# One order for all five engines, worked out by a list scheduler inside the kernel, in place of an order of matmuls written out by hand

## The chip, the cores and the metric

The kernel runs on one core of one Trainium2 chip. Such a core has five engines with queues of their own: TensorE (PE, matrix products into PSUM), VectorE (DVE), ScalarE (ACT), GpSimd (POOL) and SyncE (SP, which here issues every DMA). Each works through its own list of instructions strictly in order, and semaphores join the lists. The metric is the device time of one execution in microseconds (us), as a median over runs. A profile of one execution shows every instruction, what ended the idle time before it, and the TensorE clock that was granted.

## What is computed

Two layers. The first is a linear attention with decay, over 4 batches, 8 heads, 768 positions and 48 channels a head; the second a feed-forward layer of width 2048 with a squared ReLU, on the 3072 rows of 384 that the first gives.

```python
for t in range(S):
    cur = np.einsum('bhd,bhe->bhde', u[None] * kt, vt)
    y[:, :, t] = np.einsum('bhd,bhde->bhe', rt, state + cur)
    state = wt[:, :, :, None] * state + np.einsum('bhd,bhe->bhde', kt, vt)
x = attn_out.transpose(0, 2, 1, 3).reshape(B * S, H * D)
h = x @ w_in
r = np.maximum(h, 0.0)
out = (r * r) @ w_out
```

## The kernel before

**Steps.** Attention works on chunks of 128 positions of one batch: 6 chunks times 4 batches are 24 steps. A step loads `w`, `r`, `k` and `v` (192 KB each; L67 to L80). Its parts, with the letters that the order uses:

- `st_prep` (L144): on ACT, the logarithm of `w` into one of three `lw` buffers, and `v` cast to bf16.
- `c`, `st_cum` (L164): PE sums the logarithms along the chunk by a triangular product into the PSUM tile `cp`; ACT takes the exponent there (and of the four columns of chunk sums, `a_c`); DVE multiplies it with `r` and `k` into `rdec` (L177).
- `t`, `st_tr` (L181): eight transposes on PE into PSUM `tr`, which DVE copies to `rkT` (L189). With it goes `st_bonus` (L153), the term of `u`: POOL makes `ku` and `qprod`, DVE the sum `q` (L160), POOL `vq`.
- `p`, `st_p` (L212): products of the transposed `r` and `k`, into the same PSUM buffer `cp`; DVE masks both halves into `pmT` (L223).
- `s`, `st_su` (L191): the chunk's part of the state, into `tr`; DVE adds the old state, POOL scales it into `S` (L208). The state goes from step to step, within a batch.
- `y`, `st_y` (L227): masked products with `v`, and the state with `rkT`, into PSUM `y`; DVE adds `vq` and gives `y_sb` (L245).
- `x`, `finish` (L320): three transposes of `y_sb` into `tr`; ACT copies them into `xT` (L256).

**Products.** When the steps of a block are in `xT`, `moe_block` (L259) has its feed-forward work as units. A unit `m1` fills one PSUM bank with 512 columns of the hidden layer (6 matmuls of 256 rows in a block of two steps, 12 of 128 rows in a block of one step); ACT takes the ReLU into `rl` (L276), and DVE squares it into `gt` (L277). A unit `m2` is a quarter of the second product for 128 rows, 4 matmuls; after four of them ACT evicts `o_sb` (L291) and SP stores it (L292). There are thirteen blocks: steps 0 and 1, 2, 3, and then pairs from 4 and 5 to 22 and 23.

**Weights.** `w_in` and `w_out` come as four blocks of 768 KB each into a pool of five staging buffers, and ACT casts each block in one instruction (L100, L103).

**PSUM.** One buffer each for `cp` (two banks), `y` (two banks), `tr` and `m2` (one each) and two for `m1` fill the eight banks.

**Order.** Only the order on PE is written out (`manual_schedule` for the tensor engine, L364): strings of letters, in which `F` takes the next unit of a queue of fills. From step 3 on a step reads `c(t+1) F F x(t-1) F F t(t+1) p(t) F F s(t+1) F F y(t)`, with fewer `F` early. The units `m1` of a block alternate with the units `m2` of the block before; `LAG` holds a new block back by two fills. The other engines are ordered by the framework's own scheduler, from the order in which the instructions are written. `ahead` (L334) asks for loads up to `PF` = 8 steps ahead, into pools of 9 buffers. Loads and stores share SP's queue.

```python
f = ["F F"] * 4 if t > 8 else ["F F", "F F", "F F", "F"] if t > 5 else ["F"] * 4 if t == 3 else ["F", "", "F", ""]
run(f"c{t + 1} {f[0]}" + (f" x{t - 1}" if t > 3 else "") +
    f" {f[1]} t{t + 1} p{t} {f[2]} s{t + 1} {f[3]} y{t}")
```

Of the kernel before, what the change touches and what calls it, by code (L numbers as in the profile page):

```python
# [9 lines left out]
FP32 = mybir.dt.float32  # L10
# [7 lines left out]
def kernel(  # L18
# [11 lines left out]
    nc = tc.nc  # L30
# [14 lines left out]
    PF = 8  # L45
    LAG = 2
# [5 lines left out]
    stage_pool = ctx.enter_context(tc.tile_pool(name="stage", bufs=5))  # L52
    a_in = ctx.enter_context(tc.tile_pool(name="a_in", bufs=9))
# [45 lines left out]
    def cast_wi(g):  # L99
        nc.scalar.copy(wi_sb[:, :, g * GW:(g + 1) * GW], w_st.pop(("i", g))[:])  # L100

    def cast_wo(g):
        nc.scalar.copy(wo_sb[:, g * 4:(g + 1) * 4, :], w_st.pop(("o", g))[:])  # L103

    loads = {0: attn_load(0)}

    u_bc = consts.tile([C, H, D], FP32)
    nc.sync.dma_start(
        out=u_bc[:],
        in_=bass.AP(tensor=u.tensor, offset=u.offset,  # L110
                    ap=[[0, C]] + [list(x) for x in u.ap]))
# [13 lines left out]
    nc.vector.memset(ones_col[:], 1.0)  # L125

# [14 lines left out]
    states = {}  # L141
    S_of = {}

    def st_prep(step):  # L144

        ld = loads.pop(step)
        st = states[step] = dict(ld)
        lw = st["lw"] = lw_bufs[step % NLW]
        nc.scalar.activation(lw[:, :, 0:D], ld["w_raw"][:], AF.Ln)
        v_bf = st["v_bf"] = a_mid.tile([C, H, D], BF16, name="v_bf", bufs=3)  # L150
        nc.scalar.copy(v_bf[:], ld["v_raw"][:])  # L151

    def st_bonus(step):  # L153
        st = states[step]
        ku = a_mid.tile([C, H, D], FP32, name="ku")
        qprod = a_mid.tile([C, H, D], FP32, name="qprod")
        nc.gpsimd.tensor_mul(ku[:], st["rk_raw"][:, 1], u_bc[:])  # L157
        nc.gpsimd.tensor_mul(qprod[:], st["rk_raw"][:, 0], ku[:])  # L158
        q = a_small.tile([C, H], FP32, name="q")
        nc.vector.reduce_sum(q[:], qprod[:], axis=AX.X)  # L160
        vq = st["vq"] = a_mid.tile([C, H, D], FP32, name="vq", bufs=3)
        nc.gpsimd.tensor_mul(vq[:], st["v_raw"][:], q[:, :, None].to_broadcast([C, H, D]))  # L162

    def st_cum(step):  # L164
        st = states[step]
        lw = st["lw"]
        cs = ps_cp.tile([C, 2, 512], FP32, name="cp")
        for p in range(HP):
# [4 lines left out]
        a_c = st["a_c"] = a_small.tile([C, HP], FP32, name="a_c")  # L173
        nc.scalar.activation(a_c[:], cs[:, 0, DM:DM + HP], AF.Exp)
        nc.scalar.activation(cs[:, :, 0:DM], cs[:, :, 0:DM], AF.Exp)  # L175
        rdec = st["rdec"] = rdec_bufs[step % NRD]
        nc.vector.tensor_mul(  # L177
            rdec[:, :, :, 0:D], st["rk_raw"][:],
            cs[:, :, 0:DM].rearrange("p a (h d) -> p a h d", h=H))

    def st_tr(step):  # L181
        st = states[step]
        rdec = st["rdec"]
        ps_tr = ps_tr_pool.tile([C, 2, HP, C], BF16, name="tr")
        rkT = st["rkT"] = a_mid.tile([C, 2, HP, C], BF16, name="rkT")
        for i in range(2):
            for p in range(HP):
                nc.tensor.transpose(ps_tr[:, i, p, :], rdec[:, i, 2 * p:2 * p + 2, :], ident[:])  # L188
        nc.vector.tensor_copy(rkT[:], ps_tr[:])  # L189

    def st_su(step):  # L191
        st = states[step]
        rdec, v_bf = st["rdec"], st["v_bf"]
        c = step % NCH
        if c == NCH - 1:
            return
        ps_su = ps_tr_pool.tile([C, HP, D], FP32, name="tr")
        for p in range(HP):
            for e in range(2):
                nc.tensor.matmul(ps_su[e * DP:(e + 1) * DP, p, :], rdec[:, 1, 2 * p + e, :],  # L200
                                 v_bf[:, 2 * p + e, :], start=True, stop=True)
        t_state = a_mid.tile([C, HP, D], FP32, name="t_state")
        if c == 0:
            nc.vector.tensor_copy(t_state[:], ps_su[:])
        else:
            nc.vector.tensor_add(t_state[:], S_of[step][:], ps_su[:])  # L206
        S_new = a_mid.tile([C, HP, D], BF16, name="S", bufs=3)
        nc.gpsimd.tensor_mul(S_new[:], t_state[:],  # L208
                             st["a_c"][:, :, None].to_broadcast([C, HP, D]))
        S_of[step + 1] = S_new  # L210

    def st_p(step):  # L212
        st = states[step]
        rkT = st["rkT"]
        ps_p = ps_cp.tile([C, 2, 512], FP32, name="cp")
        pmT = st["pmT"] = a_mid.tile([C, 2, HP, C], BF16, name="pmT")
        for p in range(HP):
            for e in range(2):
# [188 lines left out]
```

## Time and profile before

| | |
|---|---|
| median of 3 runs | 233.93 us (233.86 to 234.52) |
| the profiled execution | 234.28 us |
| its span, first to last instruction | 232.5 us |
| mean granted TensorE clock | 0.955 |
| first matmul of a feed-forward unit | at 26.52 us |
| share of span in which PE was busy | 84% |
| moved by DMA | 30.42 MB |

The page of the profile gives busy time for each engine, the span in 40 slices of 5.8 us, and groups of instructions. A busy PE is not PE at its peak: matmuls overlap, and the end of each is modelled, so that the price of a unit is read from the distance between starts. `PEld` is the loading of stationary operands, which lies beside the matmuls. A group row gives the sum and the mean of one; a row of the timeline gives start, length, engine, line, operation, tiles, and in brackets the idle time ahead of it with what ended it. `SPq` rows are DMA issues: their length is the time that the queue took to accept the transfer.

### The profile page before, as it was taken

To read this page: it belongs to the slowest core of one execution; us is meant where nothing else is said; L and a number is where in the kernel's file an instruction comes from. 1 tells how busy PE (TensorE), PEld (TensorE's weight loads), DVE (VectorE), ACT (ScalarE), POOL (GpSimd) and SP (SyncE) were. 2 spreads that over 40 slices of the span, in tenths; PEclk is the share of its full clock that TensorE was granted. 3 is DMA by queue.
4 is the path that set the end of the run, shared out by engine and by line. 5 is a ranking of instruction groups with operands and counts; after the bars stand their busy time and mean duration, and the time that the engine had idled before them with its cause. 6 is when DMAs were issued, how large, how long until landed. Compare 5 with 4: busy or idle time off the path is not lost.

```text
span 232.5 us, 5432 instructions
## 1 busy us (share of the span) xinstructions
PE 194.8 (84%) x2120; PEld 141.3 (61%) x2120; DVE 143.0 (61%) x264; ACT 131.4 (57%) x249; POOL 81.2 (35%) x105
## 2 busy tenths in 40 slices
PE   0145694794787999989999999999999999999984
PEld 0023472663465677767777777777777777777742
DVE  2244356235567688796879878987677756753210
ACT  2338479274245558547655775567755664455530
POOL 4450410547525855357626563431211120000000
PEclk9999997589569999999999999999999999999999
DMA  7999998999999999998785561010001000101001
GB/s 137 206 344 280 327 295 163 190 171 189 187 206 216 174 199 194 220 184 166 141 167 113 110 126 37 34 36 3 35 34 38 35 3 34 37 34 37 34 34 68
DMA packets 107176, 30.42 MB, mean 131 GB/s; under 512 B 100368, under 2 KB 105616, under 8 KB 107152
## 3 DMA queue, kind: packets, MB, share of 16 engines
q1 hardware_dynamic: 107152, 30.09, 63.0%
q8 instruction: 16, 0.26, 0.5%
q14 instruction: 8, 0.07, 0.1%
HBM read 25.36 MB, written 4.72 MB: 129 GB/s over the span
## 4 chain that ended last, share of the span: by engine, by line
PE 56%; SPq 14%; DVE 8%; DMA 7%; POOL 6%; issue 4%; ACT 3%; POOLq 0%; DVEq 0%; ACTq 0%
SPq L68 13%; PE tr L188 4%; DMA rk_raw<-in_k_dram 4%; PE cp L220 2%; DVE pmT L223 2%; POOL qprod L158 2%; POOL ku L157 2%; DVE rkT L189 2%; DMA u_bc<-in_u_dram 2%; DMA v_raw<-in_v_dram 2%; DVE gt L277 1%; PE y L234 1%; PE tr L255 1%; PE cp L171 1%; PE m_3691 L287 1%
## 5 line engine op out<-in xcount | busy, mean ns | idle before, releaser
L277 DVE TENSOR_TENSOR gt<-rl 128x512 bf16<-128x512 f16 x96 | 48.1, 509 | 34.2 <-ACT rl L276 33.8
L272 PEld LDWEIGHTS <-wi_sb 128*128 128x128 bf16 x624 | 57.2, 102 | 15.4 <-issue 3.4
L287 PEld LDWEIGHTS <-gt 128*128 128x128 bf16 x384 | 37.4, 99 | 18.6 <-issue 2.7
L208 POOL TENSOR_TENSOR S<-t_state,a_c 128x192 bf16<-128x192 f32 x20 | 10.5, 525 | 72.6 <-DVE t_state L206 56.3
L223 DVE TENSOR_TENSOR pmT<-cp,tri_strict 128x512 bf16<-128x512 f32 x48 | 30.7, 679 | 2.5 <-PE cp L220 2.5
L162 POOL TENSOR_TENSOR vq<-v_raw,q 128x384 f32<-128x384 f32 x24 | 20.0, 833 | 32.8 <-DVE y_sb L245 18.9
L160 DVE TENSOR_REDUCE q<-qprod 128x8 f32<-128x384 f32 x24 | 13.2, 549 | 21.5 <-POOL qprod L158 13.9
L157 POOL TENSOR_TENSOR ku<-rk_raw,u_bc 128x384 f32<-128x384 f32 x24 | 24.4, 1018 | 4.6 <-DMA u_bc<-in_u_dram 4.6
L158 POOL TENSOR_TENSOR qprod<-rk_raw,ku 128x384 f32<-128x384 f32 x24 | 24.4, 1018 | 3.1 <-DVE q L160 1.3
L151 ACT CAST v_bf<-v_raw 128x384 bf16<-128x384 f32 x24 | 12.2, 510 | 15.4 <-PE y L234 8.8
L189 DVE COPY rkT<-tr 128x1024 bf16<-128x1024 bf16 x24 | 16.4, 685 | 5.7 <-PE tr L188 5.4
L175 ACT ACTIVATE cp<-cp 128x768 f32<-128x768 f32 x24 | 19.2, 799 | 0.5 <-DVE q L160 0.2
L245 DVE TENSOR_TENSOR y_sb<-vq,y 128x384 bf16<-128x384 f32 x24 | 13.2, 551 | 2.2 <-PE y L234 1.1
L256 ACT COPY xT<-tr 128x384 bf16<-128x384 bf16 x24 | 11.4, 476 | 3.4 <-PE tr L255 3.3
L220 PE MATMUL cp<-rkT 64*128 64x128 bf16 x192 | 10.6, 237 | 3.0 <-DVE rkT L189 3.0
L234 PEld LDWEIGHTS <-pmT 128*128 128x128 bf16 x192 | 8.9, 101 | 6.8 <-DVE pmT L223 4.4
L234 PE MATMUL y<-v_bf,pmT 128*128 128x48 bf16 x192 | 10.6, 191 | 2.8 <-DVE pmT L223 2.7
L177 DVE TENSOR_TENSOR rdec_buf_159<-rk_raw,cp 128x768 bf16<-128x768 f32 x8 | 7.6, 952 | 6.5 <-ACT cp L175 5.1
L255 PE MATMUL tr<-ident,y_sb 128*128 128x128 bf16 x72 | 8.6, 234 | 2.4 <-DVE y_sb L245 1.6
L220 PEld LDWEIGHTS <-rkT 64*128 64x128 bf16 x192 | 6.0, 101 | 6.2 <-DVE rkT L189 3.4
L188 PE MATMUL tr<-ident,rdec_buf_157 128*128 128x128 bf16 x64 | 5.7, 242 | 4.7 <-DVE rdec_buf_157 L177 4.7
L255 PEld LDWEIGHTS <-y_sb 128*128 128x128 bf16 x72 | 6.0, 103 | 5.9 <-DVE y_sb L245 2.8
(295 smaller groups left out, 362.8 us busy)
## 6 DMA issues: line engine op xcount, KB each, us to landing
w_raw<-in_w_dram SPq DMA_DIRECT2D x24, 192.0 KB, 4.4
rk_raw<-in_r_dram SPq DMA_DIRECT2D x24, 192.0 KB, 4.5
rk_raw<-in_k_dram SPq DMA_DIRECT2D x24, 192.0 KB, 4.6
v_raw<-in_v_dram SPq DMA_DIRECT2D x24, 192.0 KB, 4.0
out_dram<-o_sb SPq DMA_DIRECT2D x24, 192.0 KB, 2.0
w_st<-in_moe_w_in_dram SPq DMA_DIRECT2D x4, 768.0 KB, 8.0
w_st<-in_moe_w_out_dram SPq DMA_DIRECT2D x4, 768.0 KB, 9.3
u_bc<-in_u_dram SPq DMA_DIRECT2D x1, 192.0 KB, 4.2
```

What stands on the lines that cost most here:

```text
L68: nc.sync.dma_start(out=dst, in_=src[b, :, c * C:(c + 1) * C, :].rearrange("h c d -> c h d"))
L157: nc.gpsimd.tensor_mul(ku[:], st["rk_raw"][:, 1], u_bc[:])
L158: nc.gpsimd.tensor_mul(qprod[:], st["rk_raw"][:, 0], ku[:])
L162: nc.gpsimd.tensor_mul(vq[:], st["v_raw"][:], q[:, :, None].to_broadcast([C, H, D]))
L175: nc.scalar.activation(cs[:, :, 0:DM], cs[:, :, 0:DM], AF.Exp)
L189: nc.vector.tensor_copy(rkT[:], ps_tr[:])
L220: nc.tensor.matmul(ps_p[:, e, p * C:(p + 1) * C], rkT[rows, 1, p, :], rkT[rows, 0, p, :], start=True, stop=True)
L223: nc.vector.tensor_mul(pmT[:, e], ps_p[:, e].rearrange("p (a t) -> p a t", a=HP), tri_strict[:, None, :].to_broadcast([C, HP, C]))
L234: nc.tensor.matmul(ps_y[:, e, p * D:(p + 1) * D], st["pmT"][:, e, p, :], st["v_bf"][:, 2 * p + e, :], start=(p == 0), stop=(c == 0), skip_ ...
L272: nc.tensor.matmul(ps1[:, j, :], wi_sb[:, kk, n * 128:(n + 1) * 128], xT[:, kk, t0:t0 + width], start=(kk == 0), stop=(kk == KT - 1))
L277: nc.vector.tensor_mul(hold["gt"][:, g * ng:(g + 1) * ng, :], rl[:], rl[:])
L287: nc.tensor.matmul(ps2[:], gt[:, n, mt * 128:(mt + 1) * 128], wo_sb[:, n, :], start=(n == 0), stop=(n == NT - 1))
```

## The change

The order of all five engines is now worked out while the kernel is built. Every part of a step or of a block becomes an operation of its own in a table `plan`: engine, estimated length in us, rank, function, arguments, what it depends on, and which PSUM buffer (or `rl` buffer) it takes or gives back. `make_order` runs a list scheduler over it: whenever an engine is free, it takes the operation of the lowest rank whose inputs are done (0.2 us later if they come from another engine) and whose buffer is free. Attention has ranks by the step, casts 6000 and 9000, the products 10000 and up, so attention goes first. Instructions are then emitted in that order under `manual_schedule` for PE, DVE, ACT, POOL and SP.

Besides:

- The 8 casts become 28 slices (3 for a block of `w_in`, 4 for one of `w_out`); blocks 0 and 2 go to ACT, 1 and 3 to DVE. The staging pool has 8 buffers in place of 5.
- Pools of loaded inputs have 7 buffers in place of 9. The order of the loads is a fixed list.
- Ahead of the first planned `m2`, gaps of PE in the plan are filled with products of a zero tile (`warm_`), 512 columns wide, counted at 0.43 us each in the first 7 us and at 0.215 later.
- There are fourteen blocks: 0 and 1, 2, 3, 4, then pairs from 5 and 6 to 21 and 22, and 23 alone. A block's first product waits until the block three before it is done with its second.

```diff
-    PF = 8
-    LAG = 2
+    A_IN = 7
+    HOP = .2
+    PACE = 0.0
-    stage_pool = ctx.enter_context(tc.tile_pool(name="stage", bufs=5))
-    a_in = ctx.enter_context(tc.tile_pool(name="a_in", bufs=9))
+    stage_pool = ctx.enter_context(tc.tile_pool(name="stage", bufs=8))
+    a_in = ctx.enter_context(tc.tile_pool(name="a_in", bufs=A_IN))
...
-    def cast_wi(g):
-        nc.scalar.copy(wi_sb[:, :, g * GW:(g + 1) * GW], w_st.pop(("i", g))[:])
...
+    def cast(eng, kind, g, j):
+        dst = wi_sb[:, :, g * GW:(g + 1) * GW] if kind == "i" else wo_sb[:, g * 4:(g + 1) * 4, :]
+        copy = nc.scalar.copy if eng == "A" else nc.vector.tensor_copy
+        copy(dst[:, j], w_st[kind, g][:, j])
...
+    warm = consts.tile([C, 512], BF16)
+    nc.vector.memset(warm[:], 0.0)
...
+    blocks = [(0, 2), (2, 1), (3, 1), (4, 1)] + [(s, 2) for s in range(5, NSTEP - 1, 2)] + [(NSTEP - 1, 1)]
...
+    def warm_(n):
+        ps = ps_m2.tile([C, 512], FP32, name="m2")
+        for _ in range(n):
+            nc.tensor.matmul(ps[:], warm[:, 0:C], warm[:], start=True, stop=True)
...
+    for s in range(NSTEP):
+        c, at = s % NCH, s * 100
+        op("A", .52, at - 60, lw_, (s,), [("ld", s, "w")] + steps(s - NLW, "cum_"))
+        op("A", .50, at + 60, v_, (s,), [("ld", s, "v")] + steps(s - 3, "y_", "su_"))
+        op("P", .44, at, cum_, (s,), [("lw_", s)], take="cp")
+        op("A", .97, at - 90, exp_, (s,), [("cum_", s)] + steps(s - 3, "sn_"))
+        op("V", .95, at - 90, rd_, (s,), [("exp_", s), ("ld", s, "k")] + steps(s - NRD, "tr_", "su_"),
+           give="cp")
+        op("P", .52, at + 10, tr_, (s,), [("rd_", s)], take="tr")
+        op("V", .68, at - 80, rkt_, (s,), [("tr_", s)] + steps(s - 2, "y_"), give="tr")
+        op("P", .33, at + 5, p_, (s,), [("rkt_", s)], take="cp")
+        op("V", .65, at - 70, pm_, (s, 0), [("p_", s)] + steps(s - 2, "y_"))
+        op("V", .65, at - 70, pm_, (s, 1), [("pm_", s, 0)], give="cp")
...
+        op("G", 1.0, at - 50, ku_, (s,), [("ld", s, "k"), ("ld", 0, "u")] + steps(s - 2, "qp_"))
+        op("G", 1.0, at - 51, qp_, (s,), [("ku_", s)] + steps(s - 2, "q_"))
+        op("V", .55, at - 55, q_, (s,), [("qp_", s)] + steps(s - 3, "vq_"))
+        op("G", .83, at - 70, vq_, (s,), [("q_", s), ("ld", s, "v")] + steps(s - 3, "ysb_"))
...
+    for i, (s0, ns) in enumerate(blocks):
+        at, ng = 10000 + i * 1000, 4 * ns
...
+            if i >= 3:
+                deps.append(("m2_", i - 3, blocks[i - 3][1] - 1, 3))
+            op("P", .66, at + g, m1_, (i, g), deps, take="m1")
+            op("A", .60, at, rl_, (i, g), [("m1_", i, g)], take="rl", give="m1")
+            op("V", .40, at, gt_, (i, g), [("rl_", i, g)], give="rl")
...
+            op("A", .50, at - 5000, os_, (i, mt), [("m2_", i, mt, 3)], give="m2")
+            op("S", .05, -1, store, (i, mt), [("os_", i, mt)])
+
+    seq = [(0, x) for x in "wrkvu"] + [(1, x) for x in "wrkv"] + [(g, "i") for g in range(4)]
+    seq += [(2, x) for x in "wrkv"] + [(g, "o") for g in range(4)]
+    seq += [(s, x) for s in range(3, NSTEP) for x in "wrkv"]
...
+        op("S", {"i": 2.08, "o": 2.08, "u": .65}.get(x, 1.25), 0, ld, (n, x), last + free)
...
+    def make_order():
+        hop, pace, pace_from = HOP, PACE, 5
+        free_at = dict(P=0.0, V=0.0, A=1.5, G=0.0, S=2.35)
+        psum = {x: [0.0] * n for x, n in dict(cp=1, tr=1, y=1, m1=2, m2=1, rl=3).items()}
...
+        while any(todo.values()):
+            now = heapq.heappop(times)
+            for e in free_at:
+                if free_at[e] > now + 1e-6:
+                    continue
+                for key in todo[e]:
...
+        first_m2 = min(t for t, k in order if k[0] == "m2_")
+        at = 0.0
+        for t, key in [x for x in order if plan[x[1]][0] == "P"]:
+            if at < first_m2:
+                n = int((t - at - .1) / (.215 if at > 7 else .43))
+                if n > 0 and t <= first_m2:
+                    order.append((at + 1e-4, ("warm_", n)))
+            at = done[key]
+        return sorted(order, key=lambda x: x[0]), done
+
+    order, done = make_order()
+    E = mybir.EngineType
+    with tc.manual_schedule(engines={E.PE, E.DVE, E.Activation, E.Pool, E.SP}):
+        for _, key in order:
+            if key[0] == "warm_":
+                warm_(key[1])
+            else:
+                plan[key][3](*plan[key][4])
```

More of the change, by code (lines that the diff above doesn't have):

```diff
@@ L1 @@
-from collections import deque
+import heapq
 from contextlib import ExitStack
@@ L188, in st_tr, with rkt_, p_ @@
                 nc.tensor.transpose(ps_tr[:, i, p, :], rdec[:, i, 2 * p:2 * p + 2, :], ident[:])
[L189 to L216, printed above, removed]
+    def rkt_(s):
+        rkT = tiles["rkT", s] = a_mid.tile([C, 2, HP, C], BF16, name="rkT")
+        nc.vector.tensor_copy(rkT[:], tiles.pop(("tr", s))[:])
+    def p_(s):
+        rkT = tiles["rkT", s]
+        ps_p = tiles["p", s] = ps_cp.tile([C, 2, 512], FP32, name="cp")
         for p in range(HP):
@@ L320, in finish @@
-    def finish(step):
-        st_yt(step)
-        if step in blocks:
-            m1s, m2s = moe_block(*blocks[step])
-            old = held.popleft() if held else []
-            held.append(m2s)
-            units = []
-            for i in range(max(len(m1s), len(old))):
-                units += m1s[i:i + 1] + old[i:i + 1]
-            coming.append([LAG, units])
-    asked = [3]
-    def ahead(last):
-        while asked[0] <= min(last, NSTEP - 1):
-            loads[asked[0]] = attn_load(asked[0])
-            asked[0] += 1
@@ L360, in run, with xt_ @@
[L360 to L377 removed]
+    def xt_(s):
+        nc.scalar.copy(xT[:, :, s * C:(s + 1) * C], tiles.pop(("yt", s))[:])
```

355 lines of the change are left out of this document (193 added, 162 removed).

## Prediction, before the changed kernel ran

> **What bounds the kernel now.** I read the first two parts of the page, then the busy time by stretches, the timelines of TensorE (PE) and of the load queue (SP), and last the chain that ended last.
>
> ```profile
> PE 194.8 (84%) x2120; PEld 141.3 (61%) x2120; DVE 143.0 (61%) x264; ACT 131.4 (57%) x249; POOL 81.2 (35%) x105
> PEclk9999997589569999999999999999999999999999
> ```
> ```profile
> 0.00:26.50 26.50, 8.07 (x90) 5.22 (x91) 9.94 (x18) 12.05 (x16) 10.86 (x23) 1.00 1.01 246
> 26.50:75.30 48.80, 36.48 (x373) 25.97 (x373) 25.60 (x47) 26.69 (x49) 19.26 (x23) 0.79 1.12 212
> 75.30:115.00 39.70, 37.50 (x444) 27.77 (x442) 31.24 (x59) 25.31 (x52) 23.87 (x27) 1.00 1.06 187
> 115.00:154.86 39.86, 39.64 (x463) 29.14 (x461) 33.86 (x59) 25.85 (x54) 20.52 (x24) 1.00 0.41 87
> 154.86:199.51 44.65, 44.65 (x520) 33.23 (x520) 31.68 (x62) 28.00 (x56) 6.67 (x10) 1.00 0.08 29
> ```
>
> The columns are length, busy PE, weight loads, DVE, ACT, POOL, granted clock, DMA share and GB/s. From 115 us on PE has no gap: there the kernel is PE-bound, and no order can shorten it. Before 75 us PE is idle for 18.4 + 12.3 us, and part of its busy time runs at a lowered clock. So the question is how much of the first 75 us another order can fill.
>
> The price of PE work at full clock comes from the chain, at two points four steps apart:
>
> ```profile
> 154.86 0.76 PE m_2539 L272 x6
> ...
> 184.41 0.76 PE m_3088 L272 x6
> ```
>
> 29.55 us for four steps is 7.39 us a step: four units of the first product (`m1`) at 0.65, four of the second (`m2`) at 0.65, and 2.15 of attention. All 24 steps are 177.3 us.
>
> The first product begins late, and on a slow clock:
>
> ```profile
> 26.52 1.44 PE L272 MATMUL m_370<-xT,wi_sb 128*128 128x256 bf16 x6 [0.57 <-ACT xT L256]
> 27.75 1.49 PE L272 MATMUL m_380<-xT,wi_sb 128*128 128x256 bf16 x6
> ...
> 30.31 1.05 PE L272 MATMUL m_400<-xT,wi_sb 128*128 128x256 bf16 x6
> ...
> 32.10 0.82 PE L272 MATMUL m_420<-xT,wi_sb 128*128 128x256 bf16 x6
> ```
>
> Two units take 30.31 - 27.75 = 2.56 us, or 1.28 each, twice the 0.65 of the steady part: the array was at half speed although the page prints a clock of 9 there, and dense work for about 4 us woke it. So a cold start costs twice the time, and the printed clock of the first 35 us isn't proof of a warm one.
>
> Why so late? Loads and in-order waits:
>
> ```profile
> 6.66 0.51 ACT L151 CAST v_bf<-v_raw 128x384 bf16<-128x384 f32 x1 [4.64 <-DMA v_raw<-in_v_dram]
> 7.08 0.52 ACT L149 ACTIVATE lw_buf_149<-w_raw 128x384 bf16<-128x384 f32 x1
> ```
> ```profile
> 13.67 0.55 DVE L160 TENSOR_REDUCE q<-qprod 128x8 f32<-128x384 f32 x1 [2.11 <-POOL qprod L158]
> 14.14 0.68 DVE L189 COPY rkT<-tr 128x1024 bf16<-128x1024 bf16 x1
> ```
>
> The logarithm of w, loaded first, stands behind the cast of v, loaded fourth; on DVE `rkT` stands behind `q`, which waits for POOL. The loads themselves:
>
> ```profile
> 25.01 1.97 SPq L68 DMA_DIRECT2D w_raw<-in_w_dram  x1
> 27.03 4.77 SPq L68 DMA_DIRECT2D rk_raw<-in_r_dram  x1
> 31.85 3.57 SPq L68 DMA_DIRECT2D rk_raw<-in_k_dram  x1
> 35.47 0.61 SPq L68 DMA_DIRECT2D v_raw<-in_v_dram  x1
> 36.12 0.80 SPq L68 DMA_DIRECT2D w_raw<-in_w_dram  x1
> ...
> 53.02 1.15 SPq L68 DMA_DIRECT2D w_raw<-in_w_dram  x1
> ```
> ```profile
> 59.63 4.25 DMA rk_raw<-in_k_dram
> ```
>
> The first four rows are step 3; the fifth opens step 4 and the last step 8, so a step's four loads take (53.02 - 36.12) / 4 = 4.2 us, and a load lands some 4.25 us after its issue. Step 3 is therefore whole at about 40 us, and every later step 4.2 us after the one before, well under the 7.39 us that PE needs for one. Loads bound PE until about step 3, not after.
>
> **The change, part by part.** The load sequence (two steps, four `w_in` blocks, step 2, four `w_out` blocks, then steps) is the same; I cost it at nothing up to 40 us, since the queue was held by transfers, not by buffers. Arithmetic is the same. Fourteen blocks in place of thirteen mean 48 more matmuls, but the units stay 96 + 96: a unit of 12 matmuls 128 wide against 6 of 256.
>
> ```profile
> 75.34 0.83 PE L272 MATMUL m_1027<-xT,wi_sb 128*128 128x128 bf16 x12
> 76.01 0.33 PE L255 MATMUL tr<-ident,y_sb 128*128 128x128 bf16 x3
> ```
>
> The narrow unit holds PE for 76.01 - 75.34 = 0.67 us, against 0.65: 8 more such units, under 0.2 us.
>
> Floor by the loads: what can PE have done when step 3 becomes usable? The path from `rdec` to `xT` in the old order, for step 2:
>
> ```profile
> 35.70 0.95 DVE L177 TENSOR_TENSOR rdec_buf_159<-rk_raw,cp 128x768 bf16<-128x768 f32 x1 [1.70 <-ACT cp L175]
> ```
> ```profile
> 42.00 0.48 ACT L256 COPY xT<-tr 128x384 bf16<-128x384 bf16 x1 [0.81 <-PE tr L255]
> ```
>
> That is 6.8 us. So step 3's `xT` comes at 40 + 6.8, say 47 us. By then PE can have done at most steps 0 to 2 whole (22.2 us), attention of step 3 and the opening of step 4 (2.6): 24.8 us. What remains is 177.3 - 24.8 = 152.5, and PE would end at 199.5 if it never idled again. The tail stays as it is:
>
> ```profile
> 223.03 2.77 PE m_3671 L287 x16
> 226.37 2.77 PE m_3691 L287 x16
> ```
> ```profile
> 229.16 0.49 ACT L291 ACTIVATE o_sb<-m_3691 128x384 f32<-128x384 f32 x1 [2.85 <-PE m_3691 L287]
> ```
>
> Two waits of 0.6 us for `o_sb` (one `m2` buffer, unchanged), then 3.3 us from 229.16 to the end at 232.5: 4.5 us. The floor is a span of 204.0 us.
>
> To this come losses.
>
> ```profile
> 58.26 1.03 PE L188 MATMUL tr<-ident,rdec_buf_157 128*128 128x128 bf16 x8 [2.33 <-DVE rdec_buf_157 L177]
> ...
> 64.89 1.03 PE L188 MATMUL tr<-ident,rdec_buf_159 128*128 128x128 bf16 x8 [1.82 <-DVE rdec_buf_159 L177]
> ```
>
> **Feeding, 47 to 65 us: +2** (0 to 5). From 47 us steps come 4.2 us apart by loads, but all attention passes twice a step through one `cp` PSUM buffer. In the old order, with PE waiting, the transposes of two steps stood 64.89 - 58.26 = 6.6 us apart. I take 6.2 for the new order, between 4.2 and 6.6 and nearer to the row. A step brings 7.4 us of PE work, so a backlog builds, but the first two-step block, steps 5 and 6, opens only two such steps later.
>
> **Clock: +2.5** (0 to 6). The filler runs only ahead of the first planned `m2`, which can't come before a `w_out` block has landed:
>
> ```profile
> 21.66 3.30 SPq L95 DMA_DIRECT2D w_st<-in_moe_w_out_dram  x4
> ```
> ```profile
> w_st<-in_moe_w_out_dram SPq DMA_DIRECT2D x4, 768.0 KB, 9.3
> ```
>
> About 31 us, then. From there to 47 us some 12 us of work lie in 16 us.
>
> ```profile
> 60.00:65.00 5.00, 2.67 (x35) 1.55 (x35) 3.43 (x7) 2.29 (x5) 2.87 (x4) 0.50 1.13 183
> ```
>
> Here PE was busy for 2.67 of 5 us, with no gap over 2.33 us near it, and the clock was 0.50. A cold spell of 5 us does 2.5 us of work, so it costs 2.5; I take one, and two and a half at the far end.
>
> The Trainium skill, "TensorE: Matmul & The Clock Gate" (Why this matters for your kernels), asks only that no gap between bursts be longer than about 3 us. By that rule there would be no cold spell after 31 us and the sum would be 2.5 us less. The stretch at 60 us speaks against it: half the clock, without such a gap.
>
> **DVE: +2** (0 to 9).
>
> ```profile
> L277 DVE TENSOR_TENSOR gt<-rl 128x512 bf16<-128x512 f16 x96 | 48.1, 509 | 34.2 <-ACT rl L276 33.8
> ```
> ```profile
> L277 DVE TENSOR_TENSOR gt<-rl x96: 406/426/1217, 28.6 to 222.5; 128x512 bf16<-128x512 f16 x96
> ```
> ```profile
> L277 DVE TENSOR_TENSOR gt<-rl 128x512 bf16<-128x512 f16 x20 | 11.1, 564 | 0.5 <-ACT rl L276 0.5
> ```
>
> Without `gt` DVE is busy 143.0 - 48.1 = 94.9 us, 3.95 a step. In the new order attention ranks ahead of the products, so it runs as fast as `cp` allows, my 6.2 us a step. PE then has room for (6.2 - 2.15)/1.3 = 3.1 pairs of units. `gt` has a median of 0.43, but a mean of 0.56 between 75 and 115 us, where POOL was busy 60% (third row), and one took 1.22; the plan says 0.40. DVE needs 3.95 + 3.1 x 0.56 = 5.7 of 6.2 us, so it mostly keeps up. The order is fixed, however: a `gt` 0.16 late delays what is behind it. All of it for 18 steps at 3.1 each is 9 us; I take a quarter.
>
> The Trainium skill, "SBUF — State Buffer" (the shared port pair), says that a DVE operation with two SBUF inputs and a GpSimd operation exclude each other for a whole instruction. The 1.22 us of a `gt` beside a median of 0.43 agrees. By that rule a denser POOL makes more of them; it is the second rival below.
>
> **Casts: 0.** Eight whole casts on ACT become 28 slices, 14 each on ACT and DVE. On ACT the 384 wide cast of v shows 0.51 for such a slice, so 14 take 7 us, less than eight whole ones three or four times as wide. No row shows a slice on DVE. Nearest are 0.43 (`gt`) and 0.68 (`rkT`, twice as wide); I take 0.5, so 7 us (6 to 9.5) between 15 and 37 us, where DVE idles half its time: nothing on the path. PE's waiting for `w_out` covers them; were that cover gone, up to 7 us would shift.
>
> **Dummies: 0** (-0.5 to +9). No row has a 512-wide product. Four 384-wide units take 0.65 us, or 0.163 each; by width 0.22 for 512, twice that cold. They stand in gaps that PE had anyway, but PE is in order: real work that comes ready early waits behind them.
>
> **Sum:** 204.0 + 2 + 2.5 + 2 = 210.5 us of span. The profiled run took 234.28 us with a span of 232.5, so 1.8 lie around it: 212.3. That run is 0.15% above the median of 233.93, so I say 212.
>
> **The rivals.** *First: nothing is lost beyond the floor.* For it speaks the plan's lengths, close to the rows (`m1` 0.66, `rkT` 0.68 against 0.685); against it, five engines in fixed order. 204 + 1.8 + at most 1.7: 206 to 207.5.
>
> *Second: the lock between `gt` and POOL.* With DVE packed by a plan that believes 0.40, all 9 us appear on PE in place of 2, and the clock spell is whole: 212 + 7 + 2.5 = 221, 217 to 226.
>
> *Third: the dummies don't wake the array* (their operands are zeros, and no row here shows such products). Between 7 and 20 us some 9 us are gaps (13, less half of the 8.07 busy in the first stretch); filled at 0.22 a product they would take 18, and `m1` starts as late as it did: 212 + 9 = 221. It is also the way in which the change wouldn't do what it says.
>
> *Fourth, the slow side: a store ahead of the loads.*
>
> ```profile
> SPq L292 <- ACT o_sb L291: 102.1, 20, 7.3
> ```
>
> SP waits 102 us for `o_sb` in the old order and it costs nothing, since loads run up to eight steps ahead. The new order has seven buffers in place of nine, and puts loads and stores of SP in planned order. If a store whose block runs late stands ahead of a step's loads that are needed within 8.5 us (4.2 to issue, 4.25 to land), the loads come onto the path: 8.5 us a step on top of the 6.2 of attention, 7.3 over PE's need. Three such steps eat the 22 us gained, so from the fourth on the kernel is slower: 212 + 29 = 241. Against it: loads at 4.2 us gain 3 us on PE with every step.
>
> **How the numbers follow.** Forecast (207.5 to 217) 0.56; first rival 0.12; second 0.17; third 0.08; fourth 0.07, of which 0.05 ends over the old time and 0.02 near it. Measurement can tell about 0.3% from no change. Faster 0.93, same 0.02, slower 0.05. The range goes from the floor to the end of the second rival: 205 to 226.
>
> **What would show it.** First `m1` at 20 to 24 us (26.5 less some 2 for the cast of v, 1.5 for `q`, and up to 3 for waits between steps 0 and 1; the floor doesn't hang on it), with units 0.65 apart from the start (third rival: over 1 us apart, or after 25). PE gapless from about 50 us. Between 50 and 150 us DVE under 95% busy, `gt` mean under 0.6 (second rival: PE waiting for `rl` or `gt`). No load landing within 1 us ahead of its use after step 5 (fourth). PE work left at 47 us is the main assumption: if step 3 lands later than 40 us, everything shifts by as much.

## The result and the profile after

| | before | changed |
|---|---|---|
| median | 233.9 us (233.22 to 234.52) | 215.78 us (214.9 to 216.06) |
| profiled execution, and its span | 234.28, 232.5 us | 215.99, 214.2 us |
| first product unit | 26.52 us | 21.65 us |
| mean granted clock | 0.955 | 0.998 |

The ratio is 0.922 [0.9182, 0.9258]: 18 us gained, where 22 were forecast, and inside the range. Here and below a ratio leaves out runs over 1.5% above the fastest of their kernel (two of e3's, one each of e4's, e5's and e6's), while the medians count them. Two rows of the page, busy time of the engines and the granted clock in 40 slices:

```profile
PE 197.1 (92%) x2232; PEld 140.4 (66%) x2232; DVE 152.7 (71%) x279; ACT 127.5 (60%) x255; POOL 84.1 (39%) x105
PEclk9999999999999999999999999999999999999999
```

The cold stretch of the old kernel (5 to 8 tenths in five of the slices between 35 and 70 us) is gone. The stretches of the changed kernel, columns as in the prediction:

```profile
21.65:47.00 25.35, 22.88 (x242) 16.00 (x242) 16.96 (x36) 16.99 (x36) 8.48 (x10) 1.00 0.88 229
47.00:65.00 18.00, 14.59 (x242) 11.56 (x241) 15.48 (x26) 10.99 (x23) 9.82 (x11) 1.00 0.96 166
65.00:130.00 65.00, 60.95 (x734) 44.47 (x731) 57.76 (x101) 43.55 (x92) 39.63 (x44) 1.00 0.97 171
130.00:165.00 35.00, 35.00 (x436) 26.24 (x431) 30.62 (x55) 23.49 (x49) 15.61 (x19) 1.00 0.47 98
```

PE idles 18.00 - 14.59 = 3.4 us in the second stretch and 65.00 - 60.95 = 4.05 in the third; it is without a gap only from 130 us on. On PE's timeline the first products start warm, and of the two old waits for `o_sb` ahead of the last `m2` groups one is left:

```profile
21.65 1.47 PE L288 MATMUL m<-xT,wi_sb 128*128 128x256 bf16 x12 [1.02 <-ACT xT L273]
22.96 0.38 PE L321 MATMUL m<-warm 128*128 128x512 bf16 x1
...
208.07 2.76 PE L307 MATMUL m<-wo_sb,gt 128*128 128x384 bf16 x16 [0.58 <-ACT o_sb L312]
```

Two units take 22.96 - 21.65 = 1.31 us, 0.65 each, against 1.28 each in the old kernel.

**What PE had done by 47 us.** Groups of PE instructions up to 47 us (count, then busy time and mean ns):

```profile
L307 PE MATMUL m<-wo_sb,gt 128*128 128x384 bf16 x48 | 9.0, 326 | 0.1
L288 PE MATMUL m<-xT,wi_sb 128*128 128x256 bf16 x48 | 6.1, 272 | 1.0 <-ACT xT L273 1.0
L288 PE MATMUL m<-xT,wi_sb 128*128 128x128 bf16 x48 | 3.2, 219 | 1.0 <-ACT xT L273 1.0
```

That is 48/4 = 12 units `m2` and 48/6 + 48/12 = 12 units `m1`: 24 at 0.65 are 15.6 us. With the attention of steps 0 to 2 (3 x 2.15) and most of step 3 and the opening of step 4 (some 1.9, an estimate from the same groups) PE had done about 24.0 us of work, against "at most 24.8" in the prediction. What was left, 177.3 - 24.0 = 153.3, and the tail of 4.5 would have ended at 204.8 us. The span is 214.2. So 9.4 us were lost after 47 us (6.5 were allowed for): the gaps above are 3.4 and 4.05, the tail is 0.6 shorter by the wait that is gone, and 2.5 lie in no gap.

The prediction let step 3 be in `xT`, ready for PE's products, at 47 us. PE took it up at 50.98:

```profile
46.52 0.40 PE L210 MATMUL cp<-rkT 64*128 64x128 bf16 x8
...
50.98 0.83 PE L288 MATMUL m<-xT,wi_sb 128*128 128x128 bf16 x12 [0.57 <-ACT xT L273]
```

Its loads were in as forecast: its `rdec` begins at 39.73 on DVE's timeline. But in the fixed order its products `p` (first row) stand behind the sum and `rdec` of step 4, which hold the one `cp` buffer up to 46.24, and behind an `m2` group that starts at 43.82. From `rdec` to the end of `xT` at 50.93 it took 11.2 us, and not the 6.8 of the old order. PE's waits up to 50.98, of 0.24 to 0.57 us, add up to 1.6 of the 3.4 us lost in that stretch.

**The chain that ended at 54 us** (start, length, what), in part:

```profile
38.88 0.20 SPq L316
...
39.13 3.32 DMA w_raw<-in_w_dram
...
42.47 0.52 ACT lw_buf L149
42.99 0.39 ACT o_sb L312
...
43.40 0.36 SPq L316
...
43.80 2.99 DMA v_raw<-in_v_dram
...
46.81 0.51 ACT v_bf L153
47.32 0.40 ACT o_sb L312
...
47.74 0.36 SPq L316
```

This is a ring between two engines that are each in order. ACT evicts `o_sb`; SP's store (L316) waits for it; a load of `w` or `v` stands behind the store on SP; the logarithm or the cast of that load stands on ACT ahead of the next `o_sb`; and that one lets the next store go. From store to store (38.73, 43.40 and 47.74 on SP's timeline below) a turn takes 4.7 and 4.3 us, of which the load's landing is 3.3 and 3.0. These are the products that the two later evictions wait for:

```profile
41.50 0.81 PE L307 MATMUL m<-wo_sb,gt 128*128 128x384 bf16 x4
...
43.82 2.77 PE L307 MATMUL m<-wo_sb,gt 128*128 128x384 bf16 x16
```

They end at 42.31 and 46.59, and the chain has the evictions at 42.99 and 47.32. So ACT's wait for a load adds some 0.7 us to a turn; for the rest of it the store waits for its own products, with the loads behind it. On SP's own timeline the loads pause ahead of each store:

```profile
35.36 0.65 SPq L69 DMA_DIRECT2D v_raw<-in_v_dram  x1
38.73 0.36 SPq L316 DMA_DIRECT2D out_dram<-o_sb  x1
...
40.35 0.73 SPq L69 DMA_DIRECT2D rk_raw<-in_k_dram  x1
43.40 0.36 SPq L316 DMA_DIRECT2D out_dram<-o_sb  x1
...
45.02 0.58 SPq L69 DMA_DIRECT2D rk_raw<-in_r_dram  x1
47.74 0.36 SPq L316 DMA_DIRECT2D out_dram<-o_sb  x1
```

38.73 - 36.01, 43.40 - 41.08 and 47.74 - 45.60: 2.7 + 2.3 + 2.1 = 7.2 us without a load issued, just after step 3's last load. POOL's waits in the whole execution (total, times, longest) say that it lasts, and 14 of these 17, 24.8 us, lie after 47 us:

```profile
POOL ku L157 <- DMA rk_raw<-in_k_dram: 37.3, 17, 6.7
```

The pace of the loads says so too. Here `w` of step 4 goes out at 39.13 us and `w` of step 12 as below, 5.1 us a step; in the old kernel these were 36.12 and 71.32, 4.4 us a step.

```profile
80.23 0.49 SPq L69 DMA_DIRECT2D w_raw<-in_w_dram  x1
```

So the first theory (A) was that stores ahead of loads cost most of the 9.4 us. The rival (B) was the lock: DVE is 88.85 of 100 us busy between 50 and 150 us, and `gt` takes 0.70 us in the mean between 47 and 130 us, where the plan says 0.40 and the prediction 0.56:

```profile
L300 DVE TENSOR_TENSOR gt<-rl 128x512 bf16<-128x512 f16 x39 | 26.4, 701 | 1.2 <-ACT rl L295 0.9
```

The third theory (C) of the expectations is the planned order itself, with loads of 5 us a step.

### The profile page after: what moved, and what is told of

Same layout as the page of the kernel before. It is cut to its first block, busy times and chain, and to the rows that moved or that the text cites. A ratio compares the mean times of both kernels' runs of the same rounds, so it can differ in the third digit from the quotient of the medians.

```text
span 214.2 us, 5655 instructions
## 1 busy us (share of the span) xinstructions
PE 197.1 (92%) x2232; PEld 140.4 (66%) x2232; DVE 152.7 (71%) x279; ACT 127.5 (60%) x255; POOL 84.1 (39%) x105
## 4 chain that ended last, share of the span: by engine, by line
PE 46%; SPq 13%; DMA 13%; DVE 10%; issue 7%; POOL 6%; ACT 3%; DVEq 0%; POOLq 0%
PE m L307 19%; PE m L288 17%; SPq L69 10%; DMA w_st<-in_moe_w_out_dram 4%; DVE gt L300 4%; DMA w_raw<-in_w_dram 3%; DMA v_raw<-in_v_dram 3%; POOL qprod L161 2%; DVE pmT L216 2%; PE tr L198 2%; POOL ku L157 2%; DMA rk_raw<-in_r_dram 2%; POOL vq L169 2%; PE cp L210 1%; SPq L95 1%
## 5 line engine op out<-in xcount | busy, mean ns | idle before, releaser
L288 PE MATMUL m<-xT,wi_sb 128*128 128x256 bf16 (+1 forms) x672 | 76.5, 257 | 4.2 <-ACT xT L273 2.9
L295 ACT ACTIVATE rl<-m 128x512 f16<-128x512 f32 x96 | 56.5, 597 | 37.5 <-PE m L288 36.4
L307 PE MATMUL m<-wo_sb,gt 128*128 128x384 bf16 x384 | 74.9, 326 | 1.2 <-ACT o_sb L312 0.6
L300 DVE TENSOR_TENSOR gt<-rl 128x512 bf16<-128x512 f16 x96 | 54.7, 584 | 19.8 <-ACT rl L295 19.2
L157 POOL TENSOR_TENSOR ku<-rk_raw,u_bc 128x384 f32<-128x384 f32 x24 | 24.8, 1034 | 42.1 <-DMA rk_raw<-in_k_dram 37.3
L189 DVE TENSOR_TENSOR rdec_buf<-rk_raw,cp 128x768 bf16<-128x768 f32 x24 | 22.8, 948 | 11.2 <-ACT cp L185 9.0
L321 PE MATMUL m<-warm 128*128 128x512 bf16 x64 | 17.9, 416 | 1.2 <-DVE warm L129 1.2
L149 ACT ACTIVATE lw_buf<-w_raw 128x384 bf16<-128x384 f32 x24 | 12.5, 521 | 8.4 <-DMA w_raw<-in_w_dram 8.2
L312 ACT ACTIVATE o_sb<-m 128x384 f32<-128x384 f32 x24 | 11.8, 491 | 8.2 <-PE m L307 7.6
L198 PE MATMUL tr<-ident,rdec_buf 128*128 128x128 bf16 x192 | 14.8, 220 | 1.3 <-DVE rdec_buf L189 1.0
L198 PEld LDWEIGHTS <-rdec_buf 128*128 128x128 bf16 x192 | 11.5, 98 | 4.1 <-DVE rdec_buf L189 2.0
```

The lines of the kernel that those rows point to most:

```text
L157: nc.gpsimd.tensor_mul(ku[:], raw["rk", s][:, 1], u_bc[:])
L189: nc.vector.tensor_mul(rdec[:, :, :, 0:D], raw["rk", s][:], tiles.pop(("cs", s))[:, :, 0:DM].rearrange("p a (h d) -> p a h d", h=H))
L288: nc.tensor.matmul(ps1[:, j, :], wi_sb[:, kk, n * 128:(n + 1) * 128], xT[:, kk, s0 * C:s0 * C + width], start=(kk == 0), stop=(kk == KT - 1))
L295: nc.scalar.activation(rl[:], tiles.pop(("m1", i, g))[:], AF.Relu, scale=RS)
L300: nc.vector.tensor_mul(tiles["gt", i][:, g * ng:(g + 1) * ng, :], rl[:], rl[:])
L307: nc.tensor.matmul(tiles["m2"][:], gt[:, n, mt * 128:(mt + 1) * 128], wo_sb[:, n, :], start=(n == 0), stop=(n == NT - 1))
```

## The experiments

All edits are to the changed kernel, all ratios to the kernel before on the same chip. A difference of 0.01 in the ratio is 2.3 us.

| edit | median us | ratio [95%] |
|---|---|---|
| the changed kernel | 215.78 | 0.922 [0.9182, 0.9258] |
| e3, stores later | 214.45 | 0.9056 [0.8988, 0.9125] |
| e8, stores later and gaps of PE filled | 212.44 | 0.9093 [0.9061, 0.9124] |
| e13, gaps filled alone | 218.31 | 0.9314 [0.9278, 0.9349] |
| e11, less work on POOL | 217.12 | 0.9288 [0.9249, 0.9328] |
| e5, plan: `gt` 0.58 | 217.89 | 0.9282 [0.9225, 0.9339] |
| e7, plan: shorter loads | 225.11 | 0.9616 [0.9564, 0.9667] |
| e14, e8 with the lengths of loads and stores mended | 213.74 | 0.9124 [0.9094, 0.9155] |
| e1, no zero products | 218.49 | 0.9335 [0.9302, 0.9368] |
| e2, whole casts on ACT | 221.23 | 0.9476 [0.9431, 0.9521] |
| e12, e8 with whole casts | 214.46 | 0.9139 [0.9096, 0.9182] |
| e4, planned order on PE alone | 222.13 | 0.9476 [0.9431, 0.9522] |
| e6, the thirteen old blocks | 219.64 | 0.9364 [0.932, 0.9408] |

### The ring (theory A): e3, e8, e13

**e3** puts a store 6 us later in the order of SP, behind the loads that it held up, and has six output buffers in place of three:

```diff
+    STORE_LATE = 6.0
-    o_pool = ctx.enter_context(tc.tile_pool(name="moe_out", bufs=3))
+    o_pool = ctx.enter_context(tc.tile_pool(name="moe_out", bufs=6))
-                    order.append((now, key))
+                    order.append((now + (STORE_LATE if fn is store else 0), key))
```

> Each store is put into SP's order 6 us later than planned, with six output buffers in place of three; the order of every other engine is as in the changed kernel. Theory A (loads): between 36 and 130 us the steps come late because SP, working in planned order, waits for o_sb with loads behind it (2.7, 2.3 and 2.1 us between 36 and 48 alone); those 7 us of PE idling between 47 and 130 us then shrink: 211 to 214 us, and the load queue has no pause between 36 and 48 us. Theory B (DVE): the idling comes from gt, planned at 0.40 and measured at 0.58, in a fixed order; then 215 to 216.5. Theory C (the order itself, as planned with loads of 5 us a step): no change either.

The four runs took 210.85, 213.26, 215.64 and 215.99 us. The fastest is 4 us under any run of the changed kernel, but so wide a spread decides little. Two further kernels were made to be steady. **e8** also fills the gaps that the plan leaves on PE, up to 70 us, with products of the zero tile into columns of the `m2` bank that nobody reads:

```diff
+    bank = ps_m2.tile([C, 512], FP32, name="m2")
...
+    def keep_(n):
+        for _ in range(n):
+            nc.tensor.matmul(bank[:, DM:512], warm[:, 0:C], warm[:, 0:C], start=False, stop=True, skip_group_check=True)
...
+            elif at < KEEP_TO:
+                n = int((t - at - .1) / .056)
+                if n > 0:
+                    order.append((at + 1e-4, ("keep_", n)))
```

> The late stores of e3, and besides the planned gaps of PE after the first m2 and up to 70 us are filled with 128-wide products of zeros, added into the unused columns of the m2 bank. In e3 the one run with a clock of 0.999 took 210.9 us, those at 0.981 to 0.984 took 213.3 to 216.0. Theory: cold spells between 30 and 65 us make that spread; with the gaps filled the clock is over 0.99 in most runs and the time 210 to 212.5. Rival: the clock isn't what varies, or the products stand ahead of real work: 213 to 217.

All six runs kept a granted clock of 1.00 and took 211.81 to 214.03 us. On SP's timeline of e8 the loads now run on, and the first store stands behind the loads of step 4 and the first one of step 5:

```profile
36.51 0.59 SPq L72 DMA_DIRECT2D w_raw<-in_w_dram  x1
...
41.16 0.82 SPq L72 DMA_DIRECT2D w_raw<-in_w_dram  x1
42.10 0.56 SPq L319 DMA_DIRECT2D out_dram<-o_sb  x1
...
73.21 0.60 SPq L72 DMA_DIRECT2D w_raw<-in_w_dram  x1
```

The `w` of step 4, issued at 39.13 us in the changed kernel, goes out at 36.51, and that of step 12 (last row) at 73.21: 4.6 us a step for 5.1. POOL's wait for `k` falls to a third:

```profile
POOL ku L160 <- DMA rk_raw<-in_k_dram: 13.4, 3, 6.3
```

**e13** keeps the filling and takes the later stores out again, with their three added buffers. So both run at nearly the same clock and differ in the place of the stores; no `o_sb` of e13 waits for a buffer.

> The changed kernel with the gaps of PE filled up to 70 us as in e8, but with stores in their planned place. If the clock alone made e8's gain: 211.5 to 213. If the loads behind the stores made it (theory A): 214 to 216, with the clock at 1.0 and pauses of the load queue at 36, 41 and 45 us as in the changed kernel.

0.9314 against 0.9093, intervals far apart, at clocks of 0.99 to 1.00: the place of the stores costs 0.022 of 233.9, 5.2 us by the ratios and 5.9 by the medians. Theory A holds, for stores ahead of loads; whether the way back through ACT is needed for it wasn't tried alone. The loads of e13 come 5.3 us a step, counted as above (39.29 to 81.57 us). PE's busy time counts the fillers here and doesn't measure the gain; the work that is left after 130 us does. The groups of PE from there to the end, e13 first, then e8:

```profile
L309 PE MATMUL m<-wo_sb,gt 128*128 128x384 bf16 x212 | 41.4, 327 | 0.6 <-ACT o_sb L314 0.6
L290 PE MATMUL m<-xT,wi_sb 128*128 128x256 bf16 x252 | 33.6, 273 | 0.0
```
```profile
L310 PE MATMUL m<-wo_sb,gt 128*128 128x384 bf16 x204 | 39.7, 326 | 0.6 <-ACT o_sb L315 0.6
L291 PE MATMUL m<-xT,wi_sb 128*128 128x256 bf16 x234 | 31.1, 273 | 0.0
```

e8 has 8 matmuls of `m2` (two units), 18 wide ones of `m1` (three units) and, by the other groups, one step of attention less to do: 5 x 0.65 + 2.15 = 5.4 us, an estimate that agrees with the difference in time.

Filling alone makes the changed kernel slower (0.9314 against 0.922), and slower than either expectation for e13. SP's timeline of e13 has the same ring, each turn later, at 43.95 and 48.42 for 43.40 and 47.74:

```profile
43.95 0.36 SPq L318 DMA_DIRECT2D out_dram<-o_sb  x1
...
48.42 0.36 SPq L318 DMA_DIRECT2D out_dram<-o_sb  x1
```

Products that PE must work off ahead of real ones can push `o_sb` back, and with it the loads. That would account for 0.7 us by the third turn; the rest of the 2.2 isn't explained.

### The lock and the plan's lengths (theory B): e11, e5, e7, e14

**e11** takes work from POOL; it leaves out the product of `k` with `u`:

```diff
-        nc.gpsimd.tensor_mul(ku[:], raw["rk", s][:, 1], u_bc[:])
-        nc.gpsimd.tensor_mul(qp[:], raw["rk", s][:, 0], tiles.pop(("ku", s))[:])
+        nc.gpsimd.tensor_mul(qp[:], raw["rk", s][:, 0], raw["rk", s][:, 1])
-        op("G", 1.0, at - 50, ku_, (s,), [("ld", s, "k"), ("ld", 0, "u")] + steps(s - 2, "qp_"))
+        op("G", 0.01, at - 50, ku_, (s,), [("ld", s, "k"), ("ld", 0, "u")] + steps(s - 2, "qp_"))
```

> Leaves out the product of k with u on POOL (one of three long operations of a step); the plan knows it. Theory B (POOL and gt hold each other up, DVE sets PE's waits): gt's mean between 47 and 130 us falls from 0.70 us to about 0.6, DVE gains some 4 us there, and the time falls to 211 to 213.5. Theory A (loads): gt gets shorter, but the time stays at 214.5 to 216, since DVE waits for steps.

Groups of DVE between 47 and 130 us, and the stretch from 65 to 130 us, of e11:

```profile
L299 DVE TENSOR_TENSOR gt<-rl 128x512 bf16<-128x512 f16 x38 | 19.7, 537 | 2.4 <-ACT rl L294 2.2
```
```profile
65.00:130.00 65.00, 59.36 (x724) 43.19 (x722) 53.68 (x99) 41.78 (x87) 25.20 (x30) 1.00 0.91 170
```

POOL falls from 39.63 to 25.20 us, `gt` from 0.70 to 0.54, DVE from 57.76 to 53.68: `gt` is shorter with a lighter POOL, as the lock would have it. The time doesn't fall with it: 0.9288, the intervals just overlap, and its one run at a granted clock of 1.00 took 216.45 us; its median lies over both of its expectations. Its loads come 5.3 us a step (38.04 to 80.62 us), as late as before. And the fastest steady kernel, e8, has the slowest `gt` of the three:

```profile
L303 DVE TENSOR_TENSOR gt<-rl 128x512 bf16<-128x512 f16 x39 | 29.1, 773 | 0.5 <-ACT rl L298 0.4
```

So a long `gt` went with a DVE that was kept fed. Theory B falls for the changed kernel, whose end it doesn't set. "SBUF — State Buffer" of the Trainium skill (the shared port pair) says that a DVE operation with two SBUF inputs and a GpSimd operation that reads SBUF exclude each other; the fall of `gt` from 0.70 to 0.54 us agrees, while the end time shows no price for it here. Whether the lock has a price once the stores are late wasn't tried: in e8 DVE is busy 77.72 of the 83 us between 47 and 130 us.

**e5** tells the plan a `gt` of 0.58, **e7** loads of 1.05 us for 1.25, so that a step's loads take the 4.2 us read from the old trace:

```diff
-            op("V", .40, at, gt_, (i, g), [("rl_", i, g)], give="rl")
+            op("V", .58, at, gt_, (i, g), [("rl_", i, g)], give="rl")
```

> The plan counts gt at 0.58 us, its measured mean, in place of 0.40; nothing else. Theory B (DVE): the order fits the chip better and PE idles less between 47 and 130 us: 211 to 214 us. Theories A and C: 215 to 217, since DVE wasn't what PE waited for.

e5 gained nothing (0.9282; its interval touches that of the changed kernel).

```diff
-        op("S", {"i": 2.08, "o": 2.08, "u": .65}.get(x, 1.25), 0, ld, (n, x), last + free)
+        op("S", {"i": 2.08, "o": 2.08, "u": .65}.get(x, 1.05), 0, ld, (n, x), last + free)
```

> The plan counts a load of r, k, v or w at 1.05 us in place of 1.25 (4.2 us a step in place of 5, as the rows of the old kernel give); nothing else. Theories A and C: steps are planned earlier, loads stand ahead of more stores, PE's idle time after 47 us falls: 211 to 214 us. Theory B: DVE is packed no better, 215 to 217. If the chip can't deliver at 4.2 us a step beside the stores, the order is too hopeful and it gets slower, 217 to 221.

e7 cost 9 us, more than any of its expectations. Its first stretch:

```profile
21.65:47.00 25.35, 19.13 (x209) 13.58 (x209) 16.23 (x36) 16.67 (x36) 8.62 (x10) 1.00 0.91 228
```

PE is busy for 19.13 us up to 47 us where it was 22.88. A plan that expects data early puts the operations that need them early, and an in-order engine then waits with ready work behind. On e7's timelines that is so at 47.04 us: PE has waited 3.47 us for `o_sb`, which stood on ACT behind a cast of `v` that had waited 3.06 us for its load. In the changed kernel the loads came 5.1 us a step, which the plan's 1.25 a load (5.0 a step) fits better than 1.05. **e14** gives e8 the 1.05 from step 3 on and counts 0.9 us of SP for a store:

```diff
+        op("S", {"i": 2.08, "o": 2.08, "u": .65}.get(x, 1.25 if n < 3 else 1.05), 0, ld, (n, x), last + free)
+            op("S", .9, -1, store, (i, mt), [("os_", i, mt)])
```

> e8, and the plan counts a load from step 3 on at 1.05 us and a store at 0.9 on SP (measured issues), in place of 1.25 and 0.05; steps 0 to 2 stay at 1.25. If e7 got slower because its early part and its uncounted stores were too hopeful: 209 to 212. If any order that expects steps sooner than every 5 us runs into in-order waits: 215 to 221.

0.9124 against 0.9093, overlapping, and between the two expectations: with the stores late, the store's own time counted and the first steps left alone the shorter length no longer hurts, and it doesn't help. Which of the three took the harm away isn't separated. Theory C gains nothing from it.

### The other parts: e1, e2, e12, e4, e6

**e1** drops the zero products:

```diff
-                if n > 0 and t <= first_m2:
+                if n > 0 and t <= 0:
```

> The products of the zero tile are left out; the order of all else is the same. If the floor is set by loads (step 3 usable near 47 us), a cold array loses 2 to 4 us ahead of 31 us and regains part of it in the gaps before 47: 216.5 to 220, with units of the first product 1.28 us apart at the start. Rival, dummies worth nothing: 215 to 216.5. Rival, dummies carry the gain: over 222, with the granted clock low between 35 and 65 us as in the old kernel.

0.0115 or 2.7 us slower. PE's timeline of e1 begins cold: 18 matmuls, three units, take 24.68 - 21.18 = 3.5 us, 1.17 each, some 1.5 us more than warm.

```profile
21.18 3.66 PE L288 MATMUL m<-xT,wi_sb 128*128 128x256 bf16 x18 [0.56 <-ACT xT L273]
24.68 0.24 PE L176 MATMUL cp<-ones_col,lw_buf 128*128 128x1 bf16 x4
...
53.82 0.61 PE L210 MATMUL cp<-rkT 64*128 64x128 bf16 x8 [2.48 <-DVE rdec_buf L189]
```

The rest is a cold spell later. The third row waits 2.48 us for `rdec`, and the chain leads from there to a load of `k` that took 5.00 us to land and was issued behind a store. Stretches of e1, 2 us long (the granted clock is third from the end):

```profile
49.00:51.00 2.00, 0.90 (x18) 0.79 (x13) 0.56 (x2) 1.39 (x3) 0.75 (x1) 1.00 1.06 206
51.00:53.00 2.00, 0.34 (x7) 0.26 (x4) 0.19 (x1) 0.00 (x0) 0.24 (x1) 0.67 0.47 87
53.00:55.00 2.00, 1.18 (x15) 0.98 (x15) 1.30 (x2) 1.41 (x3) 2.00 (x3) 0.50 0.93 184
```

Whether the zero products ward that off or it came by chance in all four runs (clocks 0.976 to 0.984) isn't settled.

**e2** casts whole blocks again, all on ACT; **e12** does the same to e8:

```diff
-            for j in range(cols):
-                eng = "AV"[g % 2]
-                op(eng, 1.72 / cols if kind == "i" else .45, 6000 if kind == "i" else 9000,
-                   cast, (eng, kind, g, j), [("ld", g, kind)])
+            op("A", 1.48, 6000 if kind == "i" else 9000, cast, ("A", kind, g, 0), [("ld", g, kind)])
```

> The casts go back to eight whole ones on ACT (1.48 us each in the plan). As predicted (casts lie in PE's waiting for loads): 215 to 217. Rival: ACT, with 4 to 5 us more ahead of 37 us, holds up lw, exponents and xT of steps 2 and 3, and the first m2 comes later: 217 to 220.

> e8 with eight whole casts on ACT. In e2 whole casts cost 5.5 us, far over their own lengths. If that was a cascade (first m2 late, o_sb late, store late, loads behind it late, and a cold spell), it is cut off here: 212 to 214.5. If ACT's time itself holds up xT and exponents: 216.5 to 219, again some 5 us over e8.

e2 is 0.0256 or 6 us slower, over both of its expectations; e12 is only 0.0046 or 1.1 us slower than e8 (2.0 by the medians; the intervals overlap). A group of the changed kernel's DVE up to 40 us, then one of e12's ACT:

```profile
L108 DVE CAST wo_sb<-w_st 128x384 bf16<-128x384 f32 x8 | 2.5, 360 | 2.9 <-DMA w_st<-in_moe_w_out_dram 2.9
```
```profile
L111 ACT CAST wi_sb<-w_st 128x1536 bf16<-128x1536 f32 x4 | 5.9, 1472 | 4.4 <-DMA w_st<-in_moe_w_in_dram 4.4
```

A whole cast takes 1.47 us of ACT, and holds up whatever is behind. On top of e8 that is 1 to 2 us. The rest appears where the stores stand ahead of the loads: the first three of e2 go out at 39.44, 44.60 and 49.84 us, for 38.73, 43.40 and 47.74 in the changed kernel, each turn later, and a cold spell follows. e8 has neither, so which of the two carries how much isn't separated. Stretch of e2:

```profile
47.00:65.00 18.00, 13.10 (x164) 10.35 (x162) 10.43 (x18) 8.43 (x18) 8.43 (x11) 0.72 1.05 173
```

**e4** keeps the planned order on PE alone; the framework orders the other four engines:

```diff
-    with tc.manual_schedule(engines={E.PE, E.DVE, E.Activation, E.Pool, E.SP}):
+    with tc.manual_schedule(engines={E.PE}):
```

> The planned order is imposed on PE alone; ACT, DVE, POOL and SP are ordered by the framework from the same sequence of instructions. If PE's order and the dummies carry the gain: 214 to 218. If the order of the four other engines carries a part of it (stores and loads on SP, gt behind attention on DVE): 219 to 228.

0.0256 or 6 us slower, and on PE's timeline the first product is nearly back at its old place:

```profile
25.79 1.47 PE L288 MATMUL m<-xT,wi_sb 128*128 128x256 bf16 x12
```

So a third of the gain is lost with the planned order on the other engines, and it shows first in the way to the first `xT`.

**e6** puts the old blocks back:

```diff
-    blocks = [(0, 2), (2, 1), (3, 1), (4, 1)] + [(s, 2) for s in range(5, NSTEP - 1, 2)] + [(NSTEP - 1, 1)]
+    blocks = [(0, 2), (2, 1), (3, 1)] + [(s, 2) for s in range(4, NSTEP, 2)]
```

> The thirteen blocks of the old kernel (steps 4 and 5 as a pair, 22 and 23 as the last pair) in the new order; all else as in the changed kernel. By the prediction's count of units the split is worth nothing by itself: 215 to 217. If PE is short of work between 47 and 65 us, the pair 4 and 5 opens one step later than step 4 alone, and the last pair lengthens the end: 217 to 221.

0.0144 or 3.4 us slower. Step 4 now waits for step 5 before PE may use either:

```profile
21.65:47.00 25.35, 20.91 (x207) 14.92 (x210) 15.43 (x33) 16.44 (x35) 6.21 (x7) 0.93 0.78 205
```

PE is busy 2 us less up to 47 us than in the changed kernel. This profile is of a run of 221.87 us at a clock of 0.977, so it suggests the place and doesn't prove it. The last block changed as well and wasn't tried alone; from PE's last `m2` group to the end the span has 6.1 us in both kernels.

The four parts that were undone cost 6 (casts), 6 (the other engines' order), 3.4 (blocks) and 2.7 us (zero products). Each was undone alone and several act through the same late stores or the same cold spells, so the sum isn't a breakdown of the 18 us. The planned order on PE was never taken out by itself.

## Why the prediction was right, and where not

- **The bound: right. The floor: right in its sum, not in every step.** PE-bound late, load-bound early; about 24.0 us of work done by 47 us against 24.8, first `m1` at 21.65 us (20 to 24); the tail was 0.6 shorter than taken. The floor of 204.0 would be 204.8 with the work measured. But step 3 opened to PE at 50.98 us and not at 47: its path took 11.2 us where 6.8 was carried over from the old order. It isn't the ring alone, since e8 opens it at 50.06.
- **Clock +2.5: 0 in the profiled run**, and runs show 0.992 to 0.998. The gaps of the changed kernel came without a cold spell there. e1 and e2 show that it is near: 0.81 and 0.72 from 47 to 65 us.
- **Feeding +2 and DVE +2: mis-sized, and the second put down to the wrong cause.** The two stretches lost 3.4 and 4.05 us, and PE was gapless from 130 us, not from 50. The step reckoned with loads 4.2 us apart from step 3 on; they came 5.1 us apart from step 4 to 12, after 7.2 us of pauses in three turns. DVE stayed under 95%, as said, but `gt` went over 0.6 without setting the time (e11).
- **The fourth rival's mechanism, in small.** "A store ahead of the loads" was priced at 8.5 us a step and given 0.07. It is there, at 2.1 to 2.7 us of lost issue a turn, and costs 5 to 6 us in all (e13 against e8). What the prediction missed is that it comes in every turn: the plan counts a store at 0.05 us of SP, and the store stands there until its products and its eviction are done. "No load landing within 1 us ahead of its use after step 5" failed with POOL's 14 waits for `k` after 47 us.
- **Casts 0: mis-sized.** 6 us when undone, of which 1 to 2 with the stores late. The prediction costed the work and not the 1.47 us for which one cast blocks an in-order engine.
- **Dummies 0: gain of 2.7 us,** beyond the -0.5 of its bounds; the third rival was wrong, since units run 0.65 us apart from the first on. **Fourteen blocks 0: gain of 3.4 us;** the step counted units, and the wait for a block's second step (e6's profile suggests it) wasn't in it.
- **Second rival: wrong** on the time. Not settled: the 2.5 us in no gap, and why filling alone was slower by more than its ring.

For the span the terms come to 210.5 + 0.8 (floor) + 3.5 (gaps, 7.46 for 4) - 2.5 (clock) + 2.5 (in no gap) - 0.6 (tail) = 214.2 us. That the forecast lies within 4 us is in part luck: 6.8 us too little stands against 3.1 too much. e8, at 0.9093 [0.9061, 0.9124], beats the changed kernel by 0.9093/0.922, 1.4%.

## What to carry to other kernels

When loads and stores share an in-order queue, a store belongs behind the loads that the next steps need, and the place to look is a chain that goes from eviction to store to load and back into the evicting engine. In a fixed order over several engines a small error of the plan can cost much (e7 lost 9 us by 0.2 us a load), so take a length from the order that will run, and count an operation that waits on its queue for as long as it waits. A long operation on an in-order engine is priced by what stands behind it, not by its busy time.

## What the runs showed of the hardware

- Products of zeros wake the array: units 0.65 us apart from the first on with them, 1.17 without. Between products of real work they keep it awake: granted clock 1.00 in all six runs of e8, against 0.981 to 0.999 in e3, which lacks those fillers.
- In e1 the clock was 0.50 between 53 and 55 us, with no gap of PE over 2.48 us between 35 and 55 us, after a stretch in which PE was busy 0.90 + 0.34 of 4 us. "TensorE: Matmul & The Clock Gate" of the Trainium skill (Why this matters for your kernels) warns only of gaps over about 3 us; here a thin stretch was enough.
- A 384-wide slice of a cast takes 0.36 us on DVE, under the 0.5 that was estimated from other operations.
